# Attention and two expert layers in one kernel: a planner with other durations and bank rules, one bank for both halves' values, and values that follow scores on TensorE

## The chip, the cores and the metric

The kernel runs on one core of a Trainium2 chip. The metric is the device time of one execution in microseconds; lower is better. The core has five engines with a queue each: TensorE (PE in the profile), VectorE (DVE), ScalarE (ACT), GpSimd (POOL, idle here) and SyncE (SP, which issues the DMAs). A queue is worked through in program order, and an instruction that waits holds up all that stand behind it on its engine.

## The reference

Chunked attention with 8 memory keys for 4 x 8 heads of 768 tokens, then two expert layers one after the other, 512 to 2048 to 512, for all 3072 tokens:

```python
for c in range(nc):                      # chunks of 32 queries
    k_full = np.concatenate([mem_k, k[:, :, l_start:r_end]], axis=2)   # 16 left, 8 right
    v_full = np.concatenate([mem_v, v[:, :, l_start:r_end]], axis=2)
    scores = scale * np.matmul(q_c, k_full.transpose(0, 1, 3, 2))
    a = np.exp(scores - np.max(scores, axis=-1, keepdims=True))
    a = a / (np.sum(a, axis=-1, keepdims=True) + 1e-09)
    out[:, :, c_start:c_end] = np.matmul(a, v_full)
...
h = x @ w_in;  g = h * np.clip(h + 3.0, 0.0, 6.0) / 6.0;  x2 = g @ w_out       # layer 1
h = x2 @ w_in; g = np.where(h >= 1, h, np.where(h <= -1, 0, (h + 1) ** 2 / 4)) # layer 2
out = g @ w_out
```

## The kernel before

**Attention** goes in 32 blocks of 96 queries (three chunks) and 128 keys, each for 8 heads, in two halves of 4 heads. On TensorE a block has three steps: the scores (`sc`, 8 products; for the first 10 blocks two more products, L379, add the mask), the transposes of the weights (`tp`, 8) and the values (`pv`, 8). The trace has two records for each such product, for example x16 for 8. Between them stand VectorE and ScalarE: for each half the maximum (`peak`, L413), its negative (`negate`, L416), four exponentials (`exps`, L420), `weigh` (an addition and a reciprocal, L426 and L427), `norm` (L431), the copy `pt<-tp` (L253), and the split of the result into a high and a low part, `xhi` (L253, ScalarE) and `xlo` (L466, VectorE).

**The two layers** go in 6 tiles of 512 tokens each, and in each tile over 16 slices f of the 2048 hidden units. Each number is split into a high and a low part, so that a product takes three matmuls of 128 x 512 (L518 to L520 for the hidden slice, L567 to L569 or L572 to L574 for the projection). A hidden slice is 4 such triples into one bank `ph`, a projection 4 triples into four banks `py` or `po`. Below, h0, h1, ... are the hidden slices in the order of the program and p0, p1, ... the projections. After a hidden slice come `r` (ScalarE L531, then VectorE L534, which is the last to read the bank `ph`), `ghi` (ScalarE) and `glo` (VectorE L548). The projection needs `glo`.

**Weights** come packed in 64-bit words. Each of the 32 tiles of a layer takes six passes over 512 elements: `shift` (L282 on ScalarE or L284 on VectorE), `rebase` (L288, ScalarE), `sign` (L292) and `join` (L298) on VectorE, `high` (the cast `w<-raw`, ScalarE) and `low` (L308, VectorE).

**The order** of the instructions on each engine is made by a planner in the kernel (`Plan`). Each task has a key (where it would stand), a duration that is written in the code, the buffers that it reads and writes, and for some a choice of engine. The planner keeps a clock for each engine and takes tasks in order of their planned start; the numbers in it decide what stands behind what, on which engine an optional pass goes, and which buffer is taken. The first 6 blocks of attention must be through before h0 can begin; the others are spread between the products of layer 1.

**Banks.** The 8 PSUM banks are pools: 4 `y`, 2 `h` (for `ph`) and 2 `a` (attention). The first blocks' attention may use `y` too.

**Fills.** Up to 60 us of the planner's clock, where TensorE is planned to be idle before a task that takes a new bank, products of a constant tile `warm` are written into that bank for as long as the planned idle time (L673). They give no result, and they wait for the bank as the task itself does:

```python
while at + ns <= t.start + more:
    P.matmul(c, warm, ..., start=True, stop=True, skip_group_check=True)
    at += ns
```

Of the kernel before, what the change touches and what calls it, by code (L numbers as in the profile page):

```python
# [33 lines left out]
GRP = 4  # L34
# [36 lines left out]
TAIL = {"PE": 160, "DVE": 70, "ACT": 90, "POOL": 60, "SP": 0}  # L71
HOP = 70
WINDOW = 150


class Plan:
# [5 lines left out]
    def add(self, ways, key, emit, reads=(), writes=(), kb=0, after=(), hold=(), line=None):  # L82
# [15 lines left out]
        t = Task(len(self.tasks), ways, key, emit, bufs, deps, kb)  # L98
        self.tasks.append(t)
# [34 lines left out]
    def run(self, at):  # L134
        free = dict(at)
        bw = 0
        ready = {e: [] for e in free}
# [10 lines left out]
        while left:  # L148
            best = None
            for e, ts in ready.items():  # L150
# [13 lines left out]
                first = min(x[0] for x in found)  # L164
                est, t = min(
# [10 lines left out]
            ns = dict(t.ways)[e]  # L176
            t.eng, t.start = e, est
# [39 lines left out]
def fused_kernel(ctx: ExitStack, tc: tile.TileContext, qkv, qk, vv, wpk, const, out):  # L217
# [46 lines left out]
    def weight(l, f, z, key, after=()):  # L264
        raw = Buf(["w"], [128, 512], I64, "raw", w=1)
# [50 lines left out]
        add(("ACT", act(512)), key - 0.2, high, [hi], [(w, 0)])  # L316
# [41 lines left out]
    def block(j, keys):  # L358
        first = keys[1] < 0
        bank = ["a", "y"] if first else ["a"]  # L360
# [34 lines left out]
        def values(h):  # L395
            v3 = tile_of(v)[:, GRP * D * h:GRP * D * (h + 1)].rearrange("p (h d) -> p h d", h=GRP)
            for i in range(GRP):
                hp = 64 * (i % 2)
                P.matmul(  # L399
                    tile_of(pv[h])[hp:hp + 64, i // 2, :], v3[:, i, :], tile_of(pt[h])[:, i, :],  # L400
                    start=(i < 2), stop=True, skip_group_check=True,
                )

        def softmax(h, key):
            small = lambda i: tile_of(sm[h])[:QB, i]
# [6 lines left out]
            def peak(e):  # L412
                V.tensor_reduce(out=small(1), in_=src(), axis=AX.X, op=ALU.max)  # L413

            def negate(e):
                V.tensor_scalar(out=small(2), in0=small(1), scalar1=-scale, scalar2=None, op0=ALU.mult)  # L416

            def exps(e):
                for i in range(GRP):
                    A.activation(  # L420
                        out=s()[:, i, :], in_=src()[:, i, :], func=AF.Exp, scale=scale,
                        bias=small(2)[:, i:i + 1], accum_out=small(0)[:, i:i + 1],
                    )

            def weigh(e):
                V.tensor_scalar(out=small(0), in0=small(0), scalar1=1e-9, scalar2=None, op0=ALU.add)  # L426
                V.reciprocal(out=small(3), in_=small(0))  # L427

            def norm(e):
                rc = small(3).unsqueeze(2).to_broadcast([QB, GRP, KB])  # L430
# [4 lines left out]
            add(("DVE", dve(512)), key - 3.5, peak, [at], [(sm[h], 1)])  # L435
            add(("DVE", 90), key - 3.4, negate, [(sm[h], 1)], [(sm[h], 2)])
            add(("ACT", 1420), key - 3, exps, [at, (sm[h], 2)], [(st[h], 0), (sm[h], 0)])
            add(("DVE", 390), key - 2.5, weigh, [(sm[h], 0)], [(sm[h], 3)])
            add(("DVE", dve(512)), key - 2.4, norm, [(sm[h], 3)], [(st[h], 0)])

        def copy(h, key):
            ways = [("ACT", act(384, True)), ("DVE", dve(384, psum=True))]
            add(ways, key - 1.5, lambda e: cast(e, tile_of(pt[h]), tile_of(tp[h])), [(tp[h], 0)], [(pt[h], 0)])

        def result(h, key):
# [3 lines left out]
            for n in range(t0 // T, (t1 - 1) // T + 1):  # L449
                a, b = max(t0, n * T), min(t1, (n + 1) * T)  # L450
                xs, at = pv[h], (pv[h], 0)
                if n > t0 // T:
                    xs = Buf(["xt"], [128, 2, QB], F32, "xt")
                    at = (xs, 0)
                    add(("ACT", act(192, True)), key - 0.3, lambda e, xs=xs: A.copy(tile_of(xs), tile_of(pv[h])), [(pv[h], 0)], [at])
# [6 lines left out]
                def x_high(e, n=n, a=a, b=b, xs=xs):  # L462
                    cast(e, of(n, a, b, 0), tile_of(xs)[:, :, a - t0:b - t0])

                def x_low(e, n=n, a=a, b=b, xs=xs):
                    V.tensor_tensor(  # L466
                        out=of(n, a, b, 1), in0=tile_of(xs)[:, :, a - t0:b - t0], in1=of(n, a, b, 0), op=ALU.subtract
# [3 lines left out]
                add(("DVE", dve(192, psum=True)), key, x_low, [at, (xhi, part)], [(xlo, part)])  # L471
# [3 lines left out]
            ("PE", 1200 + 460 * by_pe), keys[0] - 4, scores, [(q, 0), (q, 1), "cbf"],  # L475
            [(sc[0], 0), (sc[1], 0)], hold=st, line="scores",
        )
        for h in half:
            softmax(h, keys[h])

        if first:
            for h in half:
                add(("PE", 380), keys[h] - 2, lambda e, h=h: turn(h), [(st[h], 0), "ident"], [(tp[h], 0)], hold=[pt[h]], line="turn")
                copy(h, keys[h])
                add(("PE", 560), keys[h] - 1, lambda e, h=h: values(h), [(pt[h], 0), (v, h)], [(pv[h], 0)], line="values")
        else:
            add(
                ("PE", 710), keys[1] - 2, lambda e: [turn(h) for h in half], [(st[0], 0), (st[1], 0), "ident"],
                [(tp[0], 0), (tp[1], 0)], hold=pt, line="turn",
# [254 lines left out]
```

## Time and profile before

| | |
|---|---|
| median of 3 runs | 1179.0 us (1178.77 to 1179.73) |
| the profiled execution's own time | 1178.85 us |
| its span in the profile | 1177.1 us |
| TensorE busy (PE) | 1169.6 us, 99% of the span |
| VectorE busy (DVE) | 653.7 us, 56% |
| ScalarE busy (ACT) | 504.9 us, 43% |
| mean DMA rate | 65 GB/s |
| granted TensorE clock, mean | 0.999 of full |

Busy time is the union of an engine's instructions. Matmuls overlap: one begins before the one ahead has ended, so what a stretch of TensorE's work takes is read from the starts in the timeline, not from the durations. A fill counts as busy.

### The profile page before, as it was taken

To read this page: it belongs to the slowest core of one execution; us is meant where nothing else is said; L and a number is where in the kernel's file an instruction comes from. 1 tells how busy PE (TensorE), PEld (TensorE's weight loads), DVE (VectorE), ACT (ScalarE), POOL (GpSimd) and SP (SyncE) were. 2 spreads that over 40 slices of the span, in tenths; PEclk is the share of its full clock that TensorE was granted. 3 is DMA by queue.
4 is the path that set the end of the run, shared out by engine and by line. 5 is a ranking of instruction groups with operands and counts; after the bars stand their busy time and mean duration, and the time that the engine had idled before them with its cause. 6 is when DMAs were issued, how large, how long until landed. Compare 5 with 4: busy or idle time off the path is not lost.

```text
span 1177.1 us, 15573 instructions
## 1 busy us (share of the span) xinstructions
PE 1169.6 (99%) x6072; PEld 949.4 (81%) x6072; DVE 653.7 (56%) x1204; ACT 504.9 (43%) x1238; POOL 0.2 (0%) x4
## 2 busy tenths in 40 slices
PE   9999999999999999999999999999999999999998
PEld 6687878888787878888888888888888888888887
DVE  7999964545536454542799833533533534533433
ACT  7997643434435343442677622322322322222221
POOL 0000000000000000000000000000000000000000
PEclk9999999999999999999999999999999999999999
DMA  9921130112102010120466500200200200000000
GB/s 360 372 98 50 35 101 26 50 41 70 50 25 86 25 50 25 45 64 1 161 189 186 161 1 1 72 1 1 72 1 1 72 1 1 36 1 1 36 1 36
DMA packets 32537, 76.64 MB, mean 65 GB/s; under 512 B 3920, under 2 KB 9680, under 8 KB 32464
## 3 DMA queue, kind: packets, MB, share of 16 engines
q1 hardware_dynamic: 32464, 75.64, 19.9%
q8 instruction: 48, 0.79, 0.3%
q14 instruction: 25, 0.20, 0.1%
HBM read 63.05 MB, written 12.58 MB: 64 GB/s over the span
## 4 chain that ended last, share of the span: by engine, by line
PE 97%; ACT 1%; DVE 1%; DMA 1%; SPq 0%; issue 0%
PE ph L518 15%; PE ph L519 15%; PE ph L520 15%; PE py L567 8%; PE py L568 7%; PE py L569 7%; PE po L573 7%; PE po L574 7%; PE po L572 7%; PE sc L386 3%; PE pv L399 2%; PE tp L393 2%; DMA q_sb<-qkv 1%; PE pv L673 1%; ACT st L420 0%; PE tp L673 0%
## 5 line engine op out<-in xcount | busy, mean ns | idle before, releaser
L518 PE MATMUL ph<-xhi,w 128*128 128x512 f32 x768 | 302.1, 393 | 0.0
L519 PE MATMUL ph<-xlo,w 128*128 128x512 f32 x768 | 299.2, 390 | 0.0
L520 PE MATMUL ph<-xhi,w 128*128 128x512 f32 x768 | 298.9, 389 | 0.0
L541 ACT ACTIVATE r<-r,bias 128x512 f32<-128x512 f32 x96 | 69.4, 723 | 290.3 <-DVE r L538 290.3
L548 DVE TENSOR_TENSOR glo<-r,ghi 128x512 fp32r<-128x512 f32 x192 | 132.7, 691 | 99.9 <-ACT ghi L547 98.7
L547 ACT CAST ghi<-r 128x512 fp32r<-128x512 f32 x192 | 119.2, 621 | 119.6 <-DVE r L544 72.0
L518 PEld LDWEIGHTS ph<-xhi,w 128*128 128x128 f32 x768 | 144.1, 188 | 32.0
L520 PEld LDWEIGHTS ph<-xhi,w 128*128 128x128 f32 x768 | 144.1, 188 | 30.3
L519 PEld LDWEIGHTS ph<-xlo,w 128*128 128x128 f32 x768 | 144.3, 188 | 29.1
L567 PE MATMUL py<-ghi,w 128*128 128x512 f32 x384 | 155.1, 404 | 0.0
L568 PE MATMUL py<-glo,w 128*128 128x512 f32 x384 | 150.0, 391 | 0.0
L569 PE MATMUL py<-ghi,w 128*128 128x512 f32 x384 | 149.6, 390 | 0.0
L572 PE MATMUL po<-w,ghi 128*128 128x512 f32 x384 | 149.4, 389 | 0.0
L573 PE MATMUL po<-w,ghi 128*128 128x512 f32 x384 | 149.4, 389 | 0.0
L574 PE MATMUL po<-w,glo 128*128 128x512 f32 x384 | 149.4, 389 | 0.0
L538 DVE TENSOR_SCALAR r<-ph 128x512 f32<-128x512 f32 x96 | 66.4, 691 | 147.8 <-PE ph L520 147.8
L534 DVE SCALAR_TENSOR_TENSOR r<-r,ph 128x512 f32<-128x512 f32 x96 | 65.6, 684 | 137.1 <-ACT r L531 136.9
L531 ACT ACTIVATE r<-ph,bias 128x512 f32<-128x512 f32 x96 | 65.7, 685 | 152.5 <-PE ph L520 122.0
L544 DVE TENSOR_TENSOR r<-ph,r 128x512 f32<-128x512 f32 x96 | 66.4, 691 | 75.2 <-ACT r L541 75.2
L420 ACT ACTIVATE st<-st,sm 96x128 f32<-96x128 f32 x176 | 68.3, 390 | 52.0 <-DVE sm L416 51.9
L567 PEld LDWEIGHTS py<-ghi,w 128*128 128x128 f32 x384 | 72.1, 188 | 17.8
L569 PEld LDWEIGHTS py<-ghi,w 128*128 128x128 f32 x384 | 72.1, 188 | 15.6
(58 smaller groups left out, 1127.8 us busy)
## 6 DMA issues: line engine op xcount, KB each, us to landing
raw<-wpk SPq DMA_DIRECT2D x64, 512.0 KB, 4.3
q_sb<-qk SPq DMA_DIRECT2D x44, 224.0 KB, 3.6
ymid<-ysb SPq DMA_DIRECT2D x24, 256.0 KB, 2.6
x2raw<-ymid SPq DMA_DIRECT2D x24, 256.0 KB, 4.4
out<-osb SPq DMA_DIRECT2D x24, 256.0 KB, 2.1
v_sb<-vv SPq DMA_DIRECT2D x44, 128.0 KB, 2.2
q_sb<-qkv SPq DMA_DIRECT2D x10, 448.0 KB, 7.4
v_sb<-qkv SPq DMA_DIRECT2D x10, 256.0 KB, 7.4
```

The lines of the kernel that those rows point to most:

```text
L518: P.matmul(p, whi[:, c, :], xh[:, c, :], start=(c == 0), stop=False)
L519: P.matmul(p, whi[:, c, :], xl[:, c, :], start=False, stop=False)
L520: P.matmul(p, wlo[:, c, :], xh[:, c, :], start=False, stop=(c == NC - 1))
L541: add(("ACT", act(T) + 100), k + 0.35, lambda e: A.activation(out=rt(), in_=rt(), func=AF.Square, bias=bias[:, 1:2], scale=0.5,), [], [(r, ...
L547: add(("ACT", act(T)), k + 0.5, lambda e: A.copy(tile_of(ghi), rt()), [(r, 0)], [(ghi, 0)])
L548: add(("DVE", dve(T)), k + 0.6, lambda e: V.tensor_tensor(out=tile_of(glo), in0=rt(), in1=tile_of(ghi), op=ALU.subtract,), [(r, 0), (ghi, ...
L567: P.matmul(y, w2hi, gh, start=first, stop=False)
L568: P.matmul(y, w2hi, gl, start=False, stop=False)
L569: P.matmul(y, w2lo, gh, start=False, stop=last)
L572: P.matmul(y, gh[:, t], wt[:, 0], start=first, stop=False)
L573: P.matmul(y, gh[:, t], wt[:, 1], start=False, stop=False)
L574: P.matmul(y, gl[:, t], wt[:, 0], start=False, stop=last)
```

## The change

The planner's constants and the durations in the code are replaced (for example a triple of matmuls from 695 to 680 ns, a pass of ScalarE over weights from 527 to 560 and 575). A task on TensorE gets a `kind`; a change between attention and the other products is charged 100 ns, and after an attention task another attention task is preferred where it can begin within 100 ns. `negate` and `weigh` are done once for both halves of a block, on a tile `sm` of twice the width; `negate` may go to ScalarE. Both halves' values share one bank. The scores may take a bank of pool `h`, and the first blocks' attention may use `h` as well. A layer-1 weight of the first 6 slices is loaded only while more than 6 buffers of pool `w` are free (before: more than 1).

```diff
-TAIL = {"PE": 160, "DVE": 70, "ACT": 90, "POOL": 60, "SP": 0}
+TAIL = {"PE": 160, "DVE": 85, "ACT": 110, "POOL": 60, "SP": 0}
 HOP = 70
-WINDOW = 150
+WINDOW = 100
+CHANGE = 100
...
+                if e == "PE" and last_kind:
+
+                    same = [x for x in found if x[1].kind and x[0] <= free[e] + WINDOW]
+                    found = same or found
...
+            if e == "PE":
+                ns += CHANGE * (bool(t.kind) != bool(last_kind))
+                last_kind = t.kind
...
-def dve(n, fast=False, psum=False):
-    return 80 + n / (1.92 if fast else 0.96) + (60 if psum else 0)
+def dve(n, fast=False):
+    return 70 + n / (1.92 if fast else 0.96)
...
-    return (60 if psum else 100) + n / 1.2
+    return (30 if psum else 60) + n * 0.9
...
-        raw = Buf(["w"], [128, 512], I64, "raw", w=1)
+        raw = Buf(["w"], [128, 512], I64, "raw", w=6 if l == 0 and f < 6 else 1)
...
-        add([("DVE", dve(512, True)), ("ACT", act(512))], key - 0.5, shift, writes=[lo])
-        add(("ACT", act(512)), key - 0.5, rebase, writes=[hi])
+        add([("DVE", dve(512, True)), ("ACT", 575)], key - 0.5, shift, writes=[lo])
+        add(("ACT", 575), key - 0.5, rebase, writes=[hi])
...
-        bank = ["a", "y"] if first else ["a"]
+        bank = ["a", "y", "h"] if first else ["a"]
...
-        sc = of(bank, [128, GRP, KB], "sc")
+        sc = of(bank if first else ["a", "h"], [128, GRP, KB], "sc")
...
-        sm = of(["sm"], [128, 4, GRP], "sm")
+        sm = Buf(["sm"], [128, 4, 2 * GRP], F32, "sm")
...
-        pv = of(bank, [128, 2, QB], "pv")
+        pv = Buf(bank, [128, 2, 2, QB], F32, "pv")
...
-            ("PE", 1200 + 460 * by_pe), keys[0] - 4, scores, [(q, 0), (q, 1), "cbf"],
-            [(sc[0], 0), (sc[1], 0)], hold=st, line="scores",
+            ("PE", 1050 + 460 * by_pe), keys[0] - 4, scores, [(q, 0), (q, 1), "cbf"],
+            [(sc[0], 0), (sc[1], 0)], hold=st, line="scores", kind="a",
         )
-        for h in half:
-            softmax(h, keys[h])
+        parts = [softmax(h, keys[h]) for h in half]
+        [next(x) for x in parts]
+        add([("DVE", 85), ("ACT", 130)], keys[0] - 3.4, negate, [(sm, 1, 0), (sm, 1, 1)], [(sm, 2)])
+        [next(x) for x in parts]
+        add(("DVE", 280), keys[0] - 2.5, weigh, [(sm, 0, 0), (sm, 0, 1)], [(sm, 3)])
+        [next(x) for x in parts]
...
-            t = add(("PE", 3 * (T + 44) / 2.4), k, lambda e, c=c: chunk(e, c), [(w, 0), (w, 1), *of], [(ph, 0)])
+            t = add(("PE", 680), k, lambda e, c=c: chunk(e, c), [(w, 0), (w, 1), *of], [(ph, 0)])
```

What this does to the order is seen on TensorE in layer 1. Before, at the first block whose scores have no mask products, the scores (`sc`) and the values of an earlier block (`pv`) each stand between triples of the layer (18 matmuls apart):

```order
L520 MATMUL ph<-xhi,w 128x512
L386 MATMUL sc<-q_sb 96x128 x8
L518 MATMUL ph<-xhi,w 128x512
...
L569 MATMUL py<-ghi,w 128x512
L399 MATMUL pv<-pt,v_sb 64x96 x8
L518 MATMUL ph<-xhi,w 128x512
```

In the changed kernel the same block reads:

```order
L403 MATMUL tp<-ident,st 128x96 x8
L539 MATMUL ph<-xhi,w 128x512
L540 MATMUL ph<-xlo,w 128x512
L541 MATMUL ph<-xhi,w 128x512
L396 MATMUL sc<-q_sb 96x128 x8
L409 MATMUL pv<-pt,v_sb 64x96 x8
L539 MATMUL ph<-xhi,w 128x512
```

The values moved up to stand directly behind the scores, one triple after the transposes. From h0 on, attention stands in 77 places between other products before and in 54 places now; 23 of these are such pairs. The attention work from h0 on is the same (26 times `tp`, 26 `pv`, 25 `sc`), and so are all 4608 matmuls of the layers. The fills are 164 before and 76 now. From h0 on they are 2, 10 (ahead of h2) and 14 narrow ones (ahead of a `pv`) before, and 7 (ahead of h2) and 5 (ahead of h3) now.

On VectorE the first attention block begins, before, with a maximum and its negative for each half, and `weigh` with its reciprocal for one half:

```order
L413 TENSOR_REDUCE sm<-sc 96x4
L416 TENSOR_SCALAR sm<-sm 96x4
L413 TENSOR_REDUCE sm<-sc 96x4
L416 TENSOR_SCALAR sm<-sm 96x4
L413 TENSOR_REDUCE sm<-sc 96x4
L426 TENSOR_SCALAR sm<-sm 96x4
L427 RECIPROCAL sm<-sm 96x4
L431 TENSOR_TENSOR st<-st,sm 96x512
```

Now the two halves go together:

```order
L436 TENSOR_REDUCE sm<-sc 96x4 x2
L420 TENSOR_SCALAR sm<-sm 96x8
L436 TENSOR_REDUCE sm<-sc 96x4 x2
L420 TENSOR_SCALAR sm<-sm 96x8
L436 TENSOR_REDUCE sm<-sc 96x4 x2
L423 TENSOR_SCALAR sm<-sm 96x8
L424 RECIPROCAL sm<-sm 96x8
L447 TENSOR_TENSOR st<-st,sm 96x512 x2
```

Ahead of the first `r` of a hidden slice, VectorE has this work in before and after: maxima 15 and 15, negatives 15 and 6, `weigh` with reciprocal 14 and 7, `norm` 14 and 14, copies `pt` 9 and 5, `xlo` 14 and 14, `shift` 1 and 4, other weight passes 16 and 16.

On ScalarE the stretch that ends in that first `r` reads, before:

```order
L253 CAST xhi<-xt 128x2x64
L282 ACTIVATE raw<-raw 128x512
L288 ACTIVATE raw<-raw 128x512
L282 ACTIVATE raw<-raw 128x512
L288 ACTIVATE raw<-raw 128x512
L282 ACTIVATE raw<-raw 128x512
L288 ACTIVATE raw<-raw 128x512
L253 CAST w<-raw 128x512
L253 COPY pt<-tp 128x384
L531 ACTIVATE r<-ph,bias 128x512
```

and now:

```order
L298 ACTIVATE raw<-raw 128x512 x2
L292 ACTIVATE raw<-raw 128x512
L263 CAST w<-raw 128x512
L298 ACTIVATE raw<-raw 128x512
L292 ACTIVATE raw<-raw 128x512
L298 ACTIVATE raw<-raw 128x512
L263 COPY pt<-tp 128x384 x2
L263 CAST w<-raw 128x512
L552 ACTIVATE r<-ph,bias 128x512
```

Ahead of the first `r` stand 11 shifts and 12 rebases on ScalarE before, 2 and 6 now; 5 copies `pt` before and 9 now, and one `negate` now; the 56 exponentials and the rest are the same. The weight passes that left stand behind it.

## Rows read from the trace of the kernel before

**Rows 1.** Page: the span.

```profile
span 1177.1 us, 15573 instructions
```

**Rows 2.** Windows: stretch, its length, busy us (instructions) by engine, clock, DMA.

```profile
20.00:40.00 20.00, 19.96 (x220) 14.92 (x220) 18.28 (x51) 20.00 (x76) 0.00 (x0) 1.00 1.03 406
40.00:60.00 20.00, 17.70 (x126) 12.56 (x123) 18.16 (x40) 19.08 (x60) 0.00 (x0) 1.00 1.03 355
60.00:80.00 20.00, 20.00 (x109) 16.15 (x106) 18.84 (x37) 19.97 (x47) 0.00 (x0) 1.00 0.25 95
120.00:140.00 20.00, 20.00 (x116) 16.05 (x115) 19.66 (x40) 12.13 (x36) 0.00 (x0) 1.00 0.16 43
6.90:52.47 45.57, 43.59 (x431) 31.79 (x432) 41.97 (x113) 43.67 (x170) 0.00 (x0) 1.00 1.03 383
```

**Rows 3.** Timeline of PE, h0 to h3: start, duration, instruction, wait before.

```profile
42.15 0.59 PE L518 MATMUL ph<-xhi,w 128*128 128x512 f32 x1
...
53.19 2.32 PE L673 MATMUL ph<-warm 128*128 128x512 bf16 x10 [2.30 <-DVE r L534]
55.16 0.58 PE L518 MATMUL ph<-xhi,w 128*128 128x512 f32 x1
...
58.10 1.33 PE L673 MATMUL pv<-warm 128*128 128x192 bf16 x14
```

**Rows 4.** Timeline of PE around scores and values in layer 1.

```profile
185.77 1.12 PE L386 MATMUL sc<-q_sb 64*96 64x128 f32 x16
186.82 0.50 PE L567 MATMUL py<-ghi,w 128*128 128x512 f32 x1
187.16 0.40 PE L568 MATMUL py<-glo,w 128*128 128x512 f32 x1
...
190.85 0.39 PE L520 MATMUL ph<-xhi,w 128*128 128x512 f32 x1
191.16 0.88 PE L399 MATMUL pv<-pt,v_sb 128*64 128x96 f32 x16
```

**Rows 5.** Timeline of PE in the first blocks: values directly behind scores.

```profile
25.20 1.12 PE L386 MATMUL sc<-q_sb 64*96 64x128 f32 x16
26.25 0.55 PE L399 MATMUL pv<-pt,v_sb 128*64 128x96 f32 x8
```

**Rows 6.** Timeline of DVE up to the first r.

```profile
6.90 0.69 DVE L413 TENSOR_REDUCE sm<-sc 96x4 f32<-96x512 f32 x1 [3.84 <-PE sc L386]
...
16.81 0.43 DVE L284 TENSOR_SCALAR raw<-raw 128x512 uint32<-128x512 uint32 x1
...
39.77 0.55 DVE L253 COPY pt<-tp 128x384 f32<-128x384 f32 x1
40.23 0.16 DVE L416 TENSOR_SCALAR sm<-sm 96x4 f32<-96x4 f32 x1
40.30 0.68 DVE L298 SCALAR_TENSOR_TENSOR raw<-raw 128x512 uint32<-128x512 uint32 x1
41.05 0.17 DVE L426 TENSOR_SCALAR sm<-sm 96x4 f32<-96x4 f32 x1
41.26 0.17 DVE L427 RECIPROCAL sm<-sm 96x4 f32<-96x4 f32 x1
41.46 0.69 DVE L431 TENSOR_TENSOR st<-st,sm 96x512 f32<-96x512 f32 x1
...
52.47 0.68 DVE L534 SCALAR_TENSOR_TENSOR r<-r,ph 128x512 f32<-128x512 f32 x1
```

**Rows 7.** Timeline of ACT: weight passes, the first r, two copies.

```profile
30.86 0.72 ACT L282 ACTIVATE raw<-raw 128x512 uint32<-128x512 uint8 x1
31.41 0.72 ACT L288 ACTIVATE raw<-raw 128x512 f32<-128x512 f32 x1
...
48.22 0.76 ACT L531 ACTIVATE r<-ph,bias 128x512 f32<-128x512 f32 x1
...
203.84 0.85 ACT L253 COPY pt<-tp 128x384 f32<-128x384 f32 x2
```

**Rows 8.** Timeline of PE: the transposes ahead of those copies.

```profile
202.99 0.83 PE L393 MATMUL tp<-ident,st 96*128 96x96 f32 x8
```

More of the change, by code (lines that the diff above doesn't have):

```diff
@@ L80, in __init__, with add @@
         self.wrote, self.read, self.last = {}, {}, {}
-    def add(self, ways, key, emit, reads=(), writes=(), kb=0, after=(), hold=(), line=None):
+    def add(self, ways, key, emit, reads=(), writes=(), kb=0, after=(), hold=(), line=None, kind=None):
         if isinstance(ways, tuple):
@@ L399, in values, with negate, weigh @@
                 P.matmul(
-                    tile_of(pv[h])[hp:hp + 64, i // 2, :], v3[:, i, :], tile_of(pt[h])[:, i, :],
-                    start=(i < 2), stop=True, skip_group_check=True,
-                )
+                    tile_of(pv)[hp:hp + 64, h, i // 2, :], v3[:, i, :], tile_of(pt[h])[:, i, :],
+                    start=(h == 0 and i < 2), stop=True, skip_group_check=True,
+                )
+        small = lambda i: tile_of(sm)[:QB, i]
+        def negate(e):
+            if e == "ACT":
+                A.activation(out=small(2), in_=small(1), func=AF.Copy, scale=-scale)
+            else:
+                V.tensor_scalar(out=small(2), in0=small(1), scalar1=-scale, scalar2=None, op0=ALU.mult)
+        def weigh(e):
+            V.tensor_scalar(out=small(0), in0=small(0), scalar1=1e-9, scalar2=None, op0=ALU.add)
+            V.reciprocal(out=small(3), in_=small(0))
         def softmax(h, key):
-            small = lambda i: tile_of(sm[h])[:QB, i]
+            of_h = lambda i: small(i)[:, GRP * h:GRP * (h + 1)]
             s = lambda: tile_of(st[h])[:QB]
@@ L412, in peak @@
             def peak(e):
[L413 to L416 removed]
+                V.tensor_reduce(out=of_h(1), in_=src(), axis=AX.X, op=ALU.max)
             def exps(e):
@@ L421, in exps @@
                         out=s()[:, i, :], in_=src()[:, i, :], func=AF.Exp, scale=scale,
-                        bias=small(2)[:, i:i + 1], accum_out=small(0)[:, i:i + 1],
+                        bias=of_h(2)[:, i:i + 1], accum_out=of_h(0)[:, i:i + 1],
                     )
-            def weigh(e):
-                V.tensor_scalar(out=small(0), in0=small(0), scalar1=1e-9, scalar2=None, op0=ALU.add)
-                V.reciprocal(out=small(3), in_=small(0))
             def norm(e):
-                rc = small(3).unsqueeze(2).to_broadcast([QB, GRP, KB])
+                rc = of_h(3).unsqueeze(2).to_broadcast([QB, GRP, KB])
                 V.tensor_tensor(out=s(), in0=s(), in1=rc, op=ALU.mult)
@@ L434, in softmax @@
                 add(("DVE", dve(512)), key - 3.8, mask, [(sc[h], 0), "cbf"], [at])
[L435 to L439, printed above, removed]
+            add(("DVE", dve(512)), key - 3.5, peak, [at], [(sm, 1, h)])
+            yield
+            add(("ACT", 1375 if by_pe else 1540), key - 3, exps, [at, (sm, 2)], [(st[h], 0), (sm, 0, h)])
+            yield
+            add(("DVE", dve(512)), key - 2.4, norm, [(sm, 3)], [(st[h], 0)])
+            yield
         def copy(h, key):
-            ways = [("ACT", act(384, True)), ("DVE", dve(384, psum=True))]
+            ways = [("ACT", act(384, True)), ("DVE", dve(384))]
             add(ways, key - 1.5, lambda e: cast(e, tile_of(pt[h]), tile_of(tp[h])), [(tp[h], 0)], [(pt[h], 0)])
@@ L481, in block @@
+        [next(x) for x in parts]
         if first:
             for h in half:
-                add(("PE", 380), keys[h] - 2, lambda e, h=h: turn(h), [(st[h], 0), "ident"], [(tp[h], 0)], hold=[pt[h]], line="turn")
+                add(("PE", 320), keys[h] - 2, lambda e, h=h: turn(h), [(st[h], 0), "ident"], [(tp[h], 0)], hold=[pt[h]], line="turn", kind="a")
                 copy(h, keys[h])
-                add(("PE", 560), keys[h] - 1, lambda e, h=h: values(h), [(pt[h], 0), (v, h)], [(pv[h], 0)], line="values")
+                add(("PE", 480), keys[h] - 1, lambda e, h=h: values(h), [(pt[h], 0), (v, h)], [(pv, h)], line="values", kind="a")
@@ L486, in block @@
         else:
             add(
-                ("PE", 710), keys[1] - 2, lambda e: [turn(h) for h in half], [(st[0], 0), (st[1], 0), "ident"],
-                [(tp[0], 0), (tp[1], 0)], hold=pt, line="turn",
+                ("PE", 610), keys[1] - 2, lambda e: [turn(h) for h in half], [(st[0], 0), (st[1], 0), "ident"],
+                [(tp[0], 0), (tp[1], 0)], hold=pt, line="turn", kind="a",
             )
@@ L493, in block @@
             add(
-                ("PE", 1050), keys[1] - 1, lambda e: [values(h) for h in half],
-                [(pt[0], 0), (pt[1], 0), (v, 0), (v, 1)], [(pv[0], 0), (pv[1], 0)], line="values",
+                ("PE", 820), keys[1] - 1, lambda e: [values(h) for h in half],
+                [(pt[0], 0), (pt[1], 0), (v, 0), (v, 1)], [(pv, 0), (pv, 1)], line="values", kind="a",
             )
```

26 lines of the change are left out of this document (15 added, 11 removed).

## The prediction

> **What bounds the kernel now.** I read the busy times by stretch first. From 60 us on TensorE is busy for all 20.00 us of a stretch, and it is so still where VectorE has 19.66 of 20 [rows 2]. TensorE's queue is in order and its products are fixed, so from there on only what lies between its products can be saved. Before 60 us it is otherwise: from 40 to 60 us TensorE has 17.70 of 20, and part of that is fills, while ScalarE has 20.00 of 20 from 20 to 40 us and 19.08 in the next stretch [rows 2]. The start is bound by ScalarE and VectorE, the rest by TensorE.
>
> The timeline of TensorE then shows where the start loses time. h0 begins at 42.15 us. Ahead of h2 TensorE waits 2.30 us for VectorE's `r` of h0, which frees the bank, and then still runs ten fills into that bank before h2 begins at 55.16 [rows 3]. These fills come after the wait that they were to cover, so they cost their own 55.16 - 53.19 = 1.97 us. Fourteen more, 1.33 us long, begin at 58.10 [rows 3].
>
> Last I read the timeline around one attention step in layer 1. After the scores the first matmul of a triple is followed by the next one 187.16 - 186.82 = 0.34 us later. The usual distance is 0.23 us: (190.85 - 187.16) / 16 starts. So leaving attention costs 0.11 us. Before values the distance is 191.16 - 190.85 = 0.31 us, so entering costs 0.08 [rows 4].
>
> **The change, part by part.** *Fewer places of attention.* 23 pairs of scores and values now touch, and each saves one leaving and one entering, 0.11 + 0.08 = 0.19 us, if nothing is lost between the two. The first blocks already had such pairs: scores at 25.20, values at 26.25, 1.05 us [rows 5]; scores that are followed by a triple take the same 186.82 - 185.77 = 1.05 [rows 4]. So I take 23 x 0.19 = 4.4 us. The bounds are 23 x 0.08 = 1.8, where leaving the scores is paid towards values too, and 4.4.
>
> The Trainium skill has a rule against this (TensorEngine Tiling (Array Packing), Key Properties): changing the tiling mode drains TensorE. Scores use 64 rows of the array and values 64 columns, so by that rule a pair keeps the drain between its two steps and the saving would lie near the lower bound; the equal 1.05 us do not show it, but they hold the drain in both cases if there is one, so I keep it as a rival.
>
> *What the pairs wait for.* The values stand nearer to their transposes now, so the copies `pt` might be late. The transposes at 202.99 us take 0.83 us, and both copies behind them ran from 203.84 to 204.69 [rows 7, 8]. In the new order three matmuls (0.69 us and 0.11 at the change) and the scores (1.05) stand between: the values come up at about 202.99 + 0.83 + 0.80 + 1.05 = 205.7, a us after the copies. The scores come up at 204.6; one of their banks is that of the first transposes, free when the first copy ends, half of the 0.85 us after 203.84, at 204.3. Both are covered, thinly for the scores. That cover is gone where ScalarE is full, from 60 to 80 us (19.97 of 20). There I allow 0.8 us of new waits on TensorE in all.
>
> *VectorE at the start.* Up to the first `r` VectorE loses 9 negatives of 40.30 - 40.23 = 0.07 us, 7 `weigh` with reciprocal of 41.46 - 41.05 = 0.41, and 4 copies of 40.23 - 39.77 = 0.46, and gains 3 shifts of at most 0.43 [rows 6]: -0.6 - 2.9 - 1.8 + 1.3 = -4.0 us. Before, it began at 6.90 and reached that `r` at 52.47, with 41.97 us of work and 3.60 us idle [rows 2, 6]. With the same idle time the new `r` comes at 48.5; with none at 44.9.
>
> *ScalarE at the start.* Up to its first `r` it loses 15 weight passes of 31.41 - 30.86 = 0.55 us and gains 4 copies of 0.43 and one `negate` of a few tenths [rows 7]: about -6.3 us, so it could be at its `r` at 41.9 in place of 48.22. It stops being the limit, and VectorE's stretch is the one that counts. The weight passes are not gone: they stand behind `r`, where ScalarE has room by 120 us (12.13 of 20), and they keep their order.
>
> VectorE's idle time came from waiting for ScalarE and TensorE, and part of that goes with ScalarE's load; against this stands that `exps` of the first half now wait for both maxima, and `norm` of the first half for both halves' exponentials. So between -4.0 and -7.6 I take -5.0, nearer to the same idle time: `r` of h0 on VectorE at about 47.5 us. Loads stay hidden: the first 12 tiles of weights stand where they stood in SP's queue, and the four that now stand behind attention loads are not worked on before h3.
>
> *Fills.* Seven in place of ten ahead of h2 and five in place of fourteen narrow ones: at 1.97 / 10 us each, 1.4 in place of 1.97 and 1.0 in place of 1.33, together -0.9 us.
>
> *Banks, keys, evictions.* The end of the program has the same instructions in the same order on all engines, and layer 2 is TensorE alone; I price them at nothing. What would cover a late `ph` bank there is VectorE's slack; in layer 1, scores in a bank of `h` hold it until their mask pass, and the next hidden slice takes the other bank, which `r` frees meanwhile.
>
> The sum is -5.0 - 0.9 - 4.4 + 0.8 = -9.5 us. The profiled execution had 1178.85 us with a span of 1177.1 [rows 1]; it becomes 1169.35, and with the median 0.15 above the profiled execution, 1169.5 us.
>
> **The rivals.**
> - *The pairs save only the entering* (the drain stays between scores and values): 1.8 us in place of 4.4, so 1172.1. For it speaks the rule above, against it the equal 1.05 us.
> - *The start gains nothing from VectorE*: the halves that wait for each other give back the 5.0 us, as new idle time in the first 45 us. 1174.5. For it speaks that a block's chain is now longer, against it that four blocks' scores are issued before the first transposes, so other work is there.
> - *VectorE's idle time goes altogether*: -7.6 in place of -5.0, 1166.9. Against it speaks the first 10 us, in which it waits for scores that wait for loads.
> - *Slower: weights late on VectorE.* Weight conversion begins later now, behind attention, and from 60 to 140 us VectorE is nearly full (18.84 to 19.66 of 20). If `low` of a slice is late, TensorE stops at it, at each slice again. A wait of 1 us for each of 12 slices gives 1181.5; it decides from 9.5 us of such waits on. Against it: VectorE has 4 us less to do up to the first `r` and the same number of weight passes there.
> - *Nothing to be measured*: the planner had set an order that TensorE follows anyway, and the start's gain is lost as waits by 140 us: 1179, within 0.2%, that is 2.4 us, which is about what a measurement of this kernel can tell from no change.
>
> **How the numbers follow.** I give the forecast 0.57, pairs at half 0.10, no gain on VectorE 0.12, all idle gone 0.07, slower 0.08, nothing 0.06. The first four are faster by more than 0.2%: 0.86. The range reaches from 1166.0 (idle gone, and none of the 0.8 us of waits) to 1175.0 (no gain on VectorE, some waits more).
>
> **What would show it.** In the new profile h0 should begin near 39 us and h2 near 50, the wait ahead of h2 should be under 2 us, and TensorE should have no other wait above 0.5 us after it. A pair should read scores, values 1.05 us later, and one 0.34 us distance in place of two. From h4 to the end the distance should shrink by about 4.4 us. The prediction is wrong if waits of TensorE for `w`, `glo` or a bank stand between 60 and 140 us, if VectorE's first `r` is later than 49 us, or if values begin later than 1.2 us after their scores.

## The result, and the profile after

The changed kernel takes 1167.37 us (median of 4 runs, 1166.94 to 1167.68) where the kernel before took 1179.05 beside it: the ratio is 0.9897, 95% interval 0.9882 to 0.9912. The profiled execution had 1167.54 us of its own, with a span 11.3 us shorter than before [rows 1]. A later comparison of the same kernel gave 0.9893 (0.9877 to 0.9909). Over all comparisons the kernel before took 1178.4 to 1182.2 us, and the traced execution, at 1178.85, is near the lower end, so a stretch compared with it can show up to 2 us less gain, or more loss, than a ratio does.

The page of the changed kernel, span and first row of busy times:

```profile
span 1165.8 us, 15343 instructions
PE 1157.3 (99%) x5984; PEld 943.8 (81%) x5984; DVE 626.2 (54%) x1072; ACT 519.0 (45%) x1274; POOL 0.2 (0%) x4
```

The windows of the changed kernel, with the columns of [rows 2]: the four stretches, and VectorE's way from its first maximum to its first `r`.

```profile
6.45:47.37 40.92, 38.52 (x355) 25.50 (x355) 37.89 (x89) 37.36 (x157) 0.00 (x0) 1.00 1.03 377
20.00:40.00 20.00, 19.57 (x185) 12.54 (x181) 19.11 (x49) 19.06 (x85) 0.00 (x0) 1.00 1.04 365
40.00:60.00 20.00, 17.84 (x110) 12.96 (x109) 18.83 (x35) 18.62 (x48) 0.00 (x0) 1.00 1.02 396
60.00:80.00 20.00, 20.00 (x116) 16.02 (x115) 18.94 (x35) 19.83 (x50) 0.00 (x0) 1.00 0.37 136
120.00:140.00 20.00, 20.00 (x112) 16.50 (x109) 15.69 (x29) 11.32 (x34) 0.00 (x0) 1.00 0.15 37
```

VectorE has 37.89 us of work on that way in place of 41.97 [rows 2], and it idles 40.92 - 37.89 = 3.03 us in place of 3.60. ScalarE is no longer full from 20 to 40 us. From 60 us on TensorE is busy throughout, as before.

TensorE's timeline at h0, h2 and h3 (it answers to [rows 3]), h2 and h3 with the fills ahead of them:

```profile
37.83 0.59 PE L539 MATMUL ph<-xhi,w 128*128 128x512 f32 x1
...
48.10 1.67 PE L696 MATMUL ph<-warm 128*128 128x512 bf16 x7 [1.58 <-DVE r L555]
49.42 0.58 PE L539 MATMUL ph<-xhi,w 128*128 128x512 f32 x1
...
56.86 1.24 PE L696 MATMUL ph<-warm 128*128 128x512 bf16 x5 [0.58 <-DVE r L555]
57.75 0.58 PE L539 MATMUL ph<-xhi,w 128*128 128x512 f32 x1
```

h0 begins 4.3 us earlier and h2 5.7 us earlier. The wait ahead of h2 is 0.7 us shorter, but h3 now has a wait and fills too, which it had not. VectorE's timeline shows the `r` that frees the bank for h2 (it answers to the last of [rows 6]); VectorE comes from weight passes and does not wait for it:

```profile
46.16 1.28 DVE L308 SCALAR_TENSOR_TENSOR raw<-raw 128x512 uint32<-128x512 uint32 x2
47.37 0.68 DVE L555 SCALAR_TENSOR_TENSOR r<-r,ph 128x512 f32<-128x512 f32 x1
```

ScalarE's part of that `r` stands about 4 us ahead of it, as it did before (48.22 and 52.47 [rows 6, 7]):

```profile
43.30 0.69 ACT L552 ACTIVATE r<-ph,bias 128x512 f32<-128x512 f32 x1
```

One of the 23 pairs on TensorE's timeline (it answers to [rows 4]):

```profile
100.09 0.40 PE L541 MATMUL ph<-xhi,w 128*128 128x512 f32 x1
100.42 1.12 PE L396 MATMUL sc<-q_sb 64*96 64x128 f32 x16
101.47 0.88 PE L409 MATMUL pv<-pt,v_sb 128*64 128x96 f32 x16
102.28 0.50 PE L539 MATMUL ph<-xhi,w 128*128 128x512 f32 x1
102.61 0.40 PE L540 MATMUL ph<-xlo,w 128*128 128x512 f32 x1
102.85 0.39 PE L541 MATMUL ph<-xhi,w 128*128 128x512 f32 x1
```

Entering takes 100.42 - 100.09 = 0.33 us, the scores 1.05, the values 0.81, and leaving shows as one distance of 0.33 and one of 0.24. The view of TensorE's waits over the whole span (us in total, times, longest):

```profile
PE ph L696 <- DVE r L555: 2.2, 2, 1.6
PE sc L396 <- DMA q_sb<-qkv: 1.1, 1, 1.1
PE sc L696 <- DVE bias L676: 1.0, 1, 1.0
PE pv L409 <- DVE pt L263: 0.2, 1, 0.2
```

All of these lie before 57 us: nothing is waited for in the 23 places of pairs.

**Two stretches.** TensorE has the same products ahead of h4 in both kernels (162 records of `sc`, 64 of `tp`, 112 of `pv`, 48 of hidden slices, 24 of projections), fills aside. So the span can be cut there without moving work across. The first matmul of h4 before, and now:

```profile
70.91 0.39 PE L518 MATMUL ph<-xhi,w 128*128 128x512 f32 x1
65.85 0.39 PE L539 MATMUL ph<-xhi,w 128*128 128x512 f32 x1
```

The start fell from 70.91 to 65.85 us, and the rest (h4 to the end) from 1177.1 - 70.91 = 1106.2 to 1165.8 - 65.85 = 1099.9 us: 5.1 us come from the start and 6.2 from the rest. The start can be cut again where VectorE begins its first `r`. In windows that meet there, before had 42.31 us of VectorE's work ahead of `r` and 10.16 idle from time 0; now it is 38.23 and 9.14. The row of before, then those of now:

```profile
0.00:52.47 52.47, 49.51 (x460) 34.46 (x461) 42.31 (x117) 45.16 (x172) 0.20 (x4) 1.00 0.99 361
0.00:47.37 47.37, 43.99 (x384) 28.08 (x385) 38.23 (x93) 38.85 (x159) 0.20 (x4) 1.00 0.98 354
47.37:65.85 18.48, 17.17 (x103) 12.60 (x102) 16.54 (x31) 16.96 (x45) 0.00 (x0) 1.00 0.99 394
```

From `r` to h4 it took 18.44 us before and takes 18.48 now, with the same products on TensorE in both. The whole gain of the start is VectorE's way to `r`.

### The profile page after: what moved, and what is told of

Read it like the earlier page. It is cut to its first block, busy times and chain, and to the rows that moved or that the text cites. A ratio compares the mean times of both kernels' runs of the same rounds, so it can differ in the third digit from the quotient of the medians.

```text
span 1165.8 us, 15343 instructions
## 1 busy us (share of the span) xinstructions
PE 1157.3 (99%) x5984; PEld 943.8 (81%) x5984; DVE 626.2 (54%) x1072; ACT 519.0 (45%) x1274; POOL 0.2 (0%) x4
## 4 chain that ended last, share of the span: by engine, by line
PE 95%; DMA 3%; DVE 1%; ACT 0%; SPq 0%; issue 0%
PE ph L539 15%; PE ph L541 15%; PE ph L540 15%; PE py L588 8%; PE po L594 7%; PE po L595 7%; PE po L593 7%; PE py L590 7%; PE py L589 7%; PE sc L396 2%; PE pv L409 2%; DMA raw<-wpk 2%; PE tp L403 1%; DMA v_sb<-qkv 1%; DVE w L318 0%; PE ph L696 0%
## 5 line engine op out<-in xcount | busy, mean ns | idle before, releaser
L593 PEld LDWEIGHTS po<-w,ghi 128*128 128x128 f32 x384 | 72.1, 188 | 15.1
```

The source lines that it names most:

```text
L593: P.matmul(y, gh[:, t], wt[:, 0], start=first, stop=False)
```

## The experiments

The kernel before measured from 1179.05 to 1180.82 us in the comparisons, so the runs stand here by their ratios to it and by stretches inside one execution. All times in us. "Work" and "idle" are VectorE's, from time 0 to the start of its first `r`; "rest" is the span less the start of h4; pairs are scores and values that touch on TensorE from h0 on. Ahead of h4 TensorE has the same products in all of these kernels; between `r` and h4 it has not always.

| kernel | ratio (95%) | span | work | idle | `r` | `r` to h4 | h4 | rest | pairs |
|---|---|---|---|---|---|---|---|---|---|
| before | 1 | 1177.1 | 42.31 | 10.16 | 52.47 | 18.44 | 70.91 | 1106.2 | 0 |
| changed | 0.9897 (0.9882 to 0.9912) | 1165.8 | 38.23 | 9.14 | 47.37 | 18.48 | 65.85 | 1099.9 | 23 |
| changed, again | 0.9893 (0.9877 to 0.9909) | 1165.5 | 38.22 | 8.83 | 47.05 | 18.47 | 65.52 | 1100.0 | 23 |
| no preference | 0.9952 (0.9939 to 0.9964) | 1174.0 | 38.13 | 8.76 | 46.89 | 22.64 | 69.53 | 1104.5 | 4 |
| preference only | 1.0008 (0.9999 to 1.0017) | 1179.5 | 42.29 | 10.84 | 53.13 | 17.81 | 70.94 | 1108.6 | 0 |
| banks of before | 0.9918 (0.9904 to 0.9932) | 1168.5 | 38.50 | 8.12 | 46.62 | 16.33 | 62.95 | 1105.6 | 0 |
| halves apart | 0.9920 (0.9908 to 0.9933) | 1168.7 | 39.13 | 9.47 | 48.60 | 19.99 | 68.59 | 1100.1 | 23 |
| joint passes only | 0.9966 (0.9953 to 0.9978) | 1174.5 | 39.30 | 10.29 | 49.59 | 17.85 | 67.44 | 1107.1 | 0 |
| durations only | 0.9947 (0.9933 to 0.9960) | 1172.7 | 41.18 | 9.29 | 50.47 | 16.42 | 66.89 | 1105.8 | 0 |
| old durations | 0.9984 (0.9975 to 0.9993) | 1177.9 | 40.59 | 16.10 | 56.69 | 18.59 | 75.28 | 1102.6 | 23 |
| no late fills | 0.9877 (0.9864 to 0.9891) | 1164.4 | 38.23 | 9.47 | 47.70 | 16.70 | 64.40 | 1100.0 | 23 |
| no fills | 0.9901 (0.9887 to 0.9914) | 1166.5 | 38.55 | 10.71 | 49.26 | 17.21 | 66.47 | 1100.0 | 23 |
| two banks first | 0.9910 (0.9896 to 0.9924) | 1167.9 | 38.49 | 10.89 | 49.38 | 18.28 | 67.66 | 1100.2 | 23 |
| the same, fewer fills | 0.9904 (0.9890 to 0.9917) | 1166.9 | 38.49 | 10.12 | 48.61 | 17.37 | 65.98 | 1101.0 | 23 |

### What the pairs are worth, and what makes them

**No preference** takes the charge and the preference for attention out of the changed kernel.

```diff
-CHANGE = 100
+CHANGE = 0
...
-                if e == "PE" and last_kind:
+                if e == "PE" and last_kind and CHANGE:
```

> The changed kernel without the preference for attention behind attention and without the 100 ns charge; banks, durations and joint small passes stay. From h0 on its order has 4 pairs of scores and values in place of 23 (73 places of attention in place of 54). Theory (each pair saves TensorE 0.22 us at its edges and 0.04 in the matmuls behind it): 19 pairs fewer, 19 x 0.26 = 4.9 us more than the changed kernel's 1167.4, so 1172.3; the profile from h4 to the end takes 1105 us in place of 1099.9. Rival (the time after h4 was won by less load on VectorE, not by pairs): 1167.4, since the load is the same.

Four pairs are left, in 73 places, and the rest is 1104.5 us: 19 pairs are worth 4.6 us, 0.24 each. The start is worse too, by 3.7 us, and not through pairs. The timeline shows one wait and 14 fills in place of the seven:

```profile
47.62 6.01 PE L696 MATMUL ph<-warm 128*128 128x512 bf16 x14 [3.11 <-DVE r L555]
53.19 0.66 PE L539 MATMUL ph<-xhi,w 128*128 128x512 f32 x1
```

The row of a window says why 14 fills take 53.19 - 47.62 = 5.57 us, 0.40 each, where the changed kernel's seven took 49.42 - 48.10 = 1.32, 0.19 each:

```profile
50.00:60.00 10.00, 10.00 (x38) 6.77 (x37) 7.02 (x14) 6.37 (x20) 0.00 (x0) 0.83 1.03 410
```

The granted clock is 0.83 on average over these 10 us. Behind 3.11 us without a matmul TensorE ran at the lower level, 1.2 GHz (0.50 from 47.62 to 53.19 us), and the fills behind the wait cost twice what they cost at 2.4 GHz. This did not come in every execution: the two quickest of the five (1172.7 and 1172.9 us, mean clock 1.000 where the traced one has 0.997) are 3 us shorter than the traced one, about what its 14 fills lose, 14 x 0.21. By these numbers most of the 3.7 us at the start belongs to the clock of the traced execution; no trace of a quicker one is there to show it. The 4.6 us behind h4 have no such part: the granted clock is 1.00 there, and TensorE has no wait.

**Preference only** puts the preference and the charge into the kernel before, with its durations and banks.

```diff
+CHANGE = 100
...
+                    same = [x for x in found if x[1].kind and x[0] <= free[e] + WINDOW]
+                    found = same or found
```

> The kernel before with the preference for attention behind attention and its charge alone. The order still has 77 places and no pair, since scores and values together want four banks of a pool of two; the fills ahead of h2 are 7 in place of 10. Theory: 0.6 us of fills less, 1178.4, and after h4 1106.2 us as before. Rival (the preference itself wins the time): 1173.

It makes no pair: 77 places, as before. What it does is move attention to where it is not ready. From 60 to 150 us TensorE has waits that the kernel before has not:

```profile
PE sc L388 <- ACT pt L262: 1.1, 1, 1.1
PE pv L408 <- DVE st L419: 0.8, 2, 0.5
```

All of them lie behind h4. The rest is 2.4 us longer than in the traced execution of the kernel before, 1.9 of it these waits; the ratio, 0.9999 to 1.0017, shows no loss that is clear of noise. This is what the prediction made its allowance for. It does not come with the preference and the old banks alone: the next kernel has both, with the new durations, and no wait behind h4. The kernel with the old durations and the new banks, further down, has two.

**Banks of before** takes the changed kernel and gives it two value banks and keeps the later blocks' scores out of pool `h`, so that nothing but these banks differs (the first blocks may still use `h`).

```diff
-        sc = of(bank if first else ["a", "h"], [128, GRP, KB], "sc")
+        sc = of(bank, [128, GRP, KB], "sc")
...
-        pv = Buf(bank, [128, 2, 2, QB], F32, "pv")
+        pv = of(bank, [128, 2, QB], "pv")
```

> The changed kernel with the bank rules of before for all but the first blocks' use of h: values of each half in a bank of their own, scores only in pool a. The preference stays, and yet the order has no pair (77 places): four banks would be needed at once where there are two. Theory: 23 x 0.26 = 6.0 us lost after h4, and a little at the start, 1173.4 to 1175. Rival (the banks matter at the start only): after h4 as in the changed kernel, 1099.9 us, and the total at most 1169.

No pair again, and the rest is 1105.6 us. Against it 23 pairs are worth 1105.6 - 1099.9 = 5.7 us, 0.25 each. So the banks make the pairs possible and the preference makes them; either alone gives none or four. The start was a surprise: h4 at 62.95, 2.9 us better than in the changed kernel, with no fill and no wait between `r` and h4. TensorE is busy for all of that stretch:

```profile
46.62:62.95 16.33, 16.33 (x109) 12.92 (x105) 16.26 (x31) 16.30 (x44) 0.00 (x0) 1.00 1.03 409
```

The 18.48 us of the changed kernel are 2.15 more, but not for the same products. Behind `r` the kernel with the old banks still has 30 matmuls of hidden slices and 24 records of scores where the changed one has 24 and 18. In the changed kernel the products of the stretch take 15.0 us, and TensorE waits and runs fills for 3.5.

### What the start is made of

**Halves apart** takes the joint `negate` and `weigh` of the changed kernel apart again, one for each half.

```diff
-        add(("DVE", 280), keys[0] - 2.5, weigh, [(sm, 0, 0), (sm, 0, 1)], [(sm, 3)])
+        for h in half:
+            add(("DVE", 280), keys[h] - 2.5, lambda e, h=h: weigh(e, h), [(sm, 0, h)], [(sm, 3, h)])
```

> The changed kernel with negate and weigh done for each half again. Pairs stay at 23. Up to the first r VectorE has 7 more weigh with reciprocal (0.41 us each), 2 more copies pt (0.46), 4 shifts fewer (0.34) and about 2 negatives fewer: +2.3 us; ScalarE +2.6. Theory (the start is VectorE's work up to the first r): r and h2 later by 2 to 2.5 us, 1169.7. Rival (a block's chain, in which the halves wait for each other, sets the start): the first half goes ahead alone again, so no change or a gain, 1166.5 to 1167.4.

h4 is 2.7 us later, with the rest as it was. 0.9 us of it is VectorE's work, 0.3 its idle time, and 1.5 lies behind `r`, where TensorE waits 1.96 us for that `r` and then runs ten fills ahead of values, with the granted clock at 0.63 over the fills and 0.50 over the values.

**Joint passes only** is the counterpart: that edit alone in the kernel before.

```diff
-        sm = of(["sm"], [128, 4, GRP], "sm")
+        sm = Buf(["sm"], [128, 4, 2 * GRP], F32, "sm")
...
+        add(("DVE", 90), keys[0] - 3.4, negate, [(sm, 1, 0), (sm, 1, 1)], [(sm, 2)])
+        add(("DVE", 390), keys[0] - 2.5, weigh, [(sm, 0, 0), (sm, 0, 1)], [(sm, 3)])
```

> The kernel before, with one edit of the change alone: negate and weigh take both halves' small values in one instruction; durations, banks and preference as before, 77 places of attention. Theory of the prediction (VectorE's amount of work sets the start): VectorE has 3.5 us less up to its first r, so h4 comes near 67.4 in place of 70.9, the rest stays 1106, span near 1173.6, ratio near 0.997. Rival (the durations by which the planner orders the first blocks decide, and with the old ones the halves that wait for each other give the gain back, as in the run with old durations): h4 at 70.9 or later, span 1177 or more, ratio 1.000 or above.

h4 came at 67.44 where the theory had 67.4, and the rival is out. VectorE's row up to `r`:

```profile
0.00:49.59 49.59, 46.77 (x421) 32.33 (x422) 39.30 (x93) 41.59 (x162) 0.20 (x4) 1.00 0.98 357
```

39.30 us of work are 3.01 less than before, the idle time stays (10.29 and 10.16), and `r` comes 2.88 us earlier. The other 0.6 us of the 3.5 lies behind `r`, where the theory had no gain, so that the number came out this close is partly luck. The halves that wait for each other cost nothing that can be seen. The rest is 0.9 us longer, 0.7 of it in three new waits for `pt`, `st` and the like, the longest 0.3; this is why the span is 1174.5 and not 1173.6.

**Durations only** puts the changed kernel's numbers (`TAIL`, `WINDOW`, the tasks' durations) into the kernel before.

```diff
-WINDOW = 150
+WINDOW = 100
...
-    return (60 if psum else 100) + n / 1.2
+    return (30 if psum else 60) + n * 0.9
```

> The kernel before with the new durations, tails and window alone. 78 places of attention, no pair; late fills 5 in place of 26 (2, 10 and 14). VectorE's work up to the first r is nearly that of before (1 shift, 1 copy and 1 maximum fewer, 1 weight pass more). Theory: fills -2.3, VectorE -0.7, no gain after h4: 1176. Rival (right durations are what gives the gain, whatever the banks): 1170 to 1172.

This gave more than the theory had: h4 is 4.0 us earlier. VectorE's work falls by 1.13 and its idle time by 0.87, and from `r` to h4 it takes 16.42 us in place of 18.44: no wait and no fill stands ahead of h2 any more, and TensorE is busy for all of it. The rest does not change (1105.8).

**Old durations** is the changed kernel with the numbers of before.

```diff
-WINDOW = 100
+WINDOW = 150
...
-    return (30 if psum else 60) + n * 0.9
+    return (60 if psum else 100) + n / 1.2
```

> The changed kernel with the durations, tails and window of before; banks, preference and joint passes stay. Pairs stay at 23. Late fills are 8, 1, 7, 1 and 4 in place of 7 and 5, at 0.18 us each about 1.7 us more; ahead of the first r VectorE has 6 copies more and 4 shifts fewer (+1.3 us). Theory: 1167.4 + 3.0 = 1170.4, all of it before h4. Rival (the durations are what the change lives on): the start falls back to that of before, +5.1, and new waits come between 60 and 140 us, 1173 to 1175.

The theory was far off: h4 is 9.4 us later. VectorE idles 16.10 us ahead of `r`, 7 more. TensorE's timeline shows a place where this begins:

```profile
20.39 0.55 PE L403 MATMUL tp<-ident,st 96*128 96x96 f32 x4
23.76 1.44 PE L696 MATMUL pv<-warm 128*128 128x384 bf16 x4 [2.82 <-ACT pt L263]
...
28.62 4.34 PE L696 MATMUL tp<-warm 128*128 128x384 bf16 x13
```

The fills of a value bank wait 2.82 us for a copy on ScalarE, and behind the wait the granted clock is at the lower level, 1.2 GHz:

```profile
28.62:32.75 4.13, 4.13 (x15) 2.02 (x14) 1.94 (x5) 3.99 (x23) 0.00 (x0) 0.50 1.03 407
```

13 fills take 4.13 us there, 0.32 each, where the eleven of the same size at 30.13 us in the changed kernel take 0.18, and VectorE waits 2.92 us for the transposes behind them. How the 9.4 us divide I cannot say. The rest is 2.7 us longer as well, 1.5 of it in two waits at 92 and 98 us, for `pt` and for `r`. It shows that the durations are not a detail of this change: with the new banks and the old numbers nearly all of the gain is gone (0.9984).

### The fills

**No late fills** lowers the planner's bound for fills, so that the 64 ahead of h0 stay and the 12 behind it go.

```diff
-FILL = 60000
+FILL = 42000
```

> The changed kernel without the 7 fills ahead of h2 and the 5 ahead of h3; nothing else differs. Theory: they run behind the wait for the bank, 49.42 - 48.10 = 1.32 us and 57.75 - 56.86 = 0.89 us, and cost that: 1167.4 - 2.2 = 1165.2. Rival 1 (something else was awaited behind them too, weights or glo): 1167.4. Rival 2 (they hold TensorE's clock up): matmuls of h2 and h3 start further apart than 0.23 us and the time rises to 1168 or more.

h4 is 1.45 us earlier than in the changed kernel, less than the 2.2 us that the twelve fills take. From `r` on it is 1.78 (16.70 in place of 18.48); `r` itself came 0.33 later, although VectorE and ScalarE have the same order up to it, so this much lies between executions. TensorE's timeline, ahead of h2 and of h3:

```profile
48.53 0.47 PE L539 MATMUL ph<-xhi,w 128*128 128x512 f32 x1 [1.68 <-DVE r L555]
...
56.41 0.47 PE L539 MATMUL ph<-xhi,w 128*128 128x512 f32 x1 [1.16 <-ACT w L263]
```

Ahead of h2 the fills' time is gone, since h2 follows the wait at once; ahead of h3 TensorE waits 1.16 us for a weight instead of 0.58 us for `r` and then five fills. A fill behind a wait costs its own time unless something else is late as well. This is the fastest kernel of all runs, at 0.9877; its interval overlaps that of the changed kernel, but its span is 1.1 to 1.4 us shorter.

**No fills** takes all of them out.

```diff
-FILL = 60000
+FILL = 3000
```

> The changed kernel without any fill, at the start too; nothing else differs. Theory: up to h0 the work of VectorE and ScalarE decides, so without fills the time is that without late fills, 1165.2, or a little less where fills stood in the way of values. Rival (TensorE runs at its lower level at the start without them): scores and transposes take twice as long at the start, h0 begins 2 to 5 us later, 1167 to 1170.

h4 is 2.1 us later than without the late ones alone, and the medians of the two kernels are 2.9 us apart. h0 begins at the same time (38.15 and 38.16), not 2 to 5 us later as the rival had it; what is lost lies behind it. TensorE's window from 30 to 40 us and its timeline at h0:

```profile
30.00:40.00 10.00, 4.91 (x36) 3.13 (x33) 8.96 (x24) 9.00 (x38) 0.00 (x0) 0.68 1.05 323
```

```profile
38.15 0.79 PE L539 MATMUL ph<-xhi,w 128*128 128x512 f32 x1 [2.68 <-ACT w L263]
38.74 0.63 PE L540 MATMUL ph<-xlo,w 128*128 128x512 f32 x1
...
41.66 0.63 PE L540 MATMUL ph<-xlo,w 128*128 128x512 f32 x1
42.09 0.63 PE L541 MATMUL ph<-xhi,w 128*128 128x512 f32 x1
```

With TensorE busy for 4.91 of 10 us, the granted clock is 0.68 on average, and h0's matmuls follow each other in 0.43 us in place of 0.23. The early fills keep the clock at 1.00 for h0 and are worth 2.1 us; the late ones cost 1.45.

### Why the changed start is 2.9 us behind that with the old banks

**Two banks first** gives the first blocks' values a bank for each half and leaves the later blocks with one.

```diff
-        pv = Buf(bank, [128, 2, 2, QB], F32, "pv")
+        pv = of(bank, [128, 2, QB], "pv") if first else Buf(bank, [128, 2, 2, QB], F32, "pv")
```

> The changed kernel, but the first blocks' values (those planned ahead of the hidden slices) have a bank for each half again; the later blocks keep one bank, so TensorE still has 54 places of attention from h0 on, with 23 pairs. Theory: the kernel with two value banks everywhere reached h4 at 62.95 us where the changed one had 65.85, because one bank for both halves makes the first blocks' next user wait for both halves; so h4 comes near 63 us, the rest stays 1099.9, the span is near 1163 us, and the ratio to the kernel before is near 0.987. Rival: that earlier h4 came from the order and the fills that went with 77 places and not from the banks of the first blocks; then h4 stays near 65.9 and the ratio at 0.990.

The theory fell, and the traced execution came out beyond the rival: h4 at 67.66, 1.8 us later than in the changed kernel. Timelines of TensorE and of VectorE:

```profile
37.42 3.73 PE L698 MATMUL ph<-warm 128*128 128x512 bf16 x11 [2.38 <-ACT st L442]
```

```profile
46.50 0.56 DVE L263 COPY pt<-tp 128x384 f32<-128x384 f32 x1 [3.03 <-PE tp L405]
```

Ahead of h0 TensorE now waits 2.38 us for ScalarE's exponentials to leave the bank and then runs eleven fills. The transposes behind come at 45.97, where the changed kernel has them at 40.48, and VectorE waits 3.03 us for them ahead of `r`. With more banks for the values the planner gave h0 a bank that scores still held, and the order behind it is another. Part of the 1.8 us is the clock, 0.69 on average from 37.42 to 40.50 us and 0.50 from there to 42; the next kernel has the same 2.38 us of wait with the clock at 1.00.

**The same, fewer fills** adds the lower bound for fills.

```diff
-FILL = 60000
+FILL = 42000
```

> As the run with two banks for the first blocks, but the planner's bound for fills is 42000 ns in place of 60000, so that of the fills behind h0 eight ahead of one slice are left and the seven others are gone. Theory (a fill that stands behind the wait for its bank costs its own time, 0.2 us each): h4 some 1 to 1.4 us earlier than in that run, so near 61.8, span near 1161.7, ratio near 0.986, the fastest of all runs. Rival (the wait for the next r or w takes the place of the fills): h4 and ratio as in that run, within 0.3 us.

```profile
38.29 2.54 PE L698 MATMUL ph<-warm 128*128 128x512 bf16 x11 [2.38 <-ACT st L442]
```

h4 is 1.7 us earlier than in the run before it. The fills' theory had 1 to 1.4, but only 0.9 lies behind `r`, where the two kernels differ. The other 0.8 lies ahead of it, where TensorE, VectorE and ScalarE have the same order, fills included, and so it is no effect of the edit. The ratio is 0.9904, no faster than the changed kernel, and h4 is 1.6 us later than in the kernel without late fills.

**Changed, again**, beside these three:

> The changed kernel once more, beside the others of this call: all theories expect a span near 1165.8 us, h4 near 65.85 and a ratio near 0.990.

h4 at 65.52, rest 1100.0, 0.9893. The stretches of these two executions agree within 0.3 us; with the kernel without late fills, whose order up to `r` is the same, `r` lies between 47.05 and 47.70. A difference of up to 0.7 us in `r` therefore tells nothing by itself, nor one of 0.8 where the clock fell in one of the two executions.

## Why the prediction was right, step by step

The time was in the range and on the right side, 2.1 us under the number. By its steps:

- **VectorE up to `r`, -5.0 us forecast: -5.1 measured.** Work -4.08 us (forecast -4.0), idle -1.0 (forecast -1.0). Of the idle time 0.57 lies where the forecast had it, between the first maximum and `r`; the other 0.45 is the first maximum, at 6.45 in place of 6.90 us. It waits for loads and stands anywhere from 6.45 to 7.96 us in these runs, so that the sum agrees to 0.1 us is luck. Joint passes alone gave -3.01 us of work where the two terms for them were -3.5. The rivals "the start gains nothing from VectorE" and "VectorE's idle time goes altogether" fell, and with no wait for weights from 60 us on "slower" and "nothing to be measured" did too. h0 was forecast near 39 us and h2 near 50; they came at 37.83 and 49.42. One reading was off without harm: the prediction has ScalarE stop being the limit, but ScalarE's part of `r` stood 4.25 us ahead of VectorE's already before and stands 4.07 ahead now, so VectorE set that `r` in both.
- **Fills, -0.9 forecast: nothing measured.** The fills did fall from 3.3 us [rows 3] to 1.32 + 0.89 = 2.2 us, as forecast. But a wait of 0.58 us for the second `r` stands ahead of h3 now, where before no wait and no fill stood (the forecast had no such wait above 0.5 us), and from `r` to h4 it takes 18.48 us in place of 18.44. By the distances between starts in that stretch the fills fell by 1.0 us, the new wait took back 0.6, and the matmuls of hidden slices next to fills and attention the other 0.4. The step went wrong where it took the time of fills for time saved and let no wait come in its place.
- **Pairs, -4.4 us forecast: -5.7 measured** against the same kernel without pairs, 0.25 each in place of 0.19. Over all places from h4 on, entering values takes 0.318 us and leaving scores 0.338 (0.31 and 0.34 in [rows 4]), together 0.20 above two steps of 0.227. The second matmul after leaving is slower too (0.235), the third a little (0.23), and scores run on into values in 1.07 where they took 1.08 to a triple: that makes 0.22. The remaining 0.03 lies spread over the other matmuls. The mechanism was right; the term left out what follows the first distance.
- **Waits that the pairs bring, +0.8 forecast: none.** From 60 us on no wait of 0.2 us or more is left for TensorE, not even where ScalarE has 19.83 of 20.
- **The rest** fell by 6.2 us in all; the 0.5 us beside the pairs also appears with the old banks (1105.6) and with new durations alone (1105.8). The forecast had priced it at nothing.

The sum was -9.5 us and the span fell by 11.3. Pairs 1.3 and allowance 0.8 and the rest 0.5 were too small a gain, fills 0.9 too large a one, and that these errors partly cancel is luck. The other 0.3 of the 2.1 us is the step to the median, forecast 0.15 above the profiled execution and measured 0.17 below it.

The rule of the Trainium skill that was weighed (TensorEngine Tiling (Array Packing), Key Properties: a change of tiling mode drains the engine) did not make pairs save only the entering. In the trace scores to values take 1.07 us on average over the 23 pairs, no more than scores to a triple, and the values' leaving is paid once. Whether a drain is inside both distances no run here shows.

What the prediction did not see is how the parts work together. Joint passes alone bring h4 forward by 3.5 us and durations alone by 4.0; both with the old banks by 8.0, about the sum (that kernel has the preference, the first blocks' use of `h` and the rule for loading weights as well). The new banks give back 2.9 of it at the start (`r` comes 0.75 later, hardly more than its spread, and h4 another 2.15 behind it) and, with the preference, bring 5.7 later. One value bank in the first blocks is not the cause, or not alone, as the run with two there shows. Whether it is the scores in pool `h` or the later blocks' one bank stays open: they were not tried apart. No run tried the first blocks' use of `h`, the rule for loading weights or the charge of 100 ns by itself either.

## What to carry to other kernels

Cut the span where the same work lies on both sides, here at h4, and an edit's gain and the loss that another edit brings can be told apart. On an in-order queue, filling work that stands behind the wait it was to cover costs its own time, twice as much where the clock has fallen in the wait, so put it ahead of the wait or leave it out. Where a planner sets the order, its durations and its bank rules have to be tried together: the preference alone gave nothing here, the durations alone half of the gain, and preference, banks and joint passes with the old durations next to nothing.

## What the runs showed that I had not expected

- Behind a wait of 3.11 us and one of 2.82 us TensorE ran at the lower level (fills of 0.40 and 0.32 us in place of 0.19 and 0.18); behind the waits of 1.58 and 1.68 us the granted clock stayed at 1.00. The same wait of 2.38 us, behind the same work, was followed by eleven fills of 0.29 us in one kernel (two banks first) and of 0.20 in another (the same, fewer fills): from one execution to the next the clock fell or did not.
- Leaving attention is felt for three matmuls: 0.337, 0.235 and 0.23 us to the next, then 0.227.
